# Half of the first token block by plain matmuls, the other half by Strassen after the second block

## The chip, the cores and the metric

The kernel runs on one core of a Trainium2 chip. The core has several engines, each with its own instruction queue that it works through in order: TensorE (PE, matmuls), VectorE (DVE), ScalarE (ACT), GpSimd (POOL) and SyncE (SP, which here only issues DMAs). PE accumulates matmuls in PSUM banks; the other data lies in SBUF, and inputs and outputs in DRAM. The metric is the time of one execution in microseconds (us), less is better.

## The reference

`q`, `k` and `v` are float32 of shape (8 batches, 8 heads, 576 positions, 64); the weights `w_in` (512 x 2048) and `w_out` (2048 x 512) lie in DRAM as float64.

```python
kv  = einsum('bhsd,bhse->bhde', k, v)
out = einsum('bhsd,bhde->bhse', q, kv)
rms = sqrt(mean(out * out, axis=-1, keepdims=True) + 1e-06)
x   = (out / rms * g_norm)       # heads side by side: 4608 tokens x 512
h   = x @ w_in                   # 4608 x 2048
g   = maximum(0.01 * h, h)
return g @ w_out                 # 4608 x 512
```

The two matmuls with the weights are nearly all of the arithmetic.

## The kernel before

**Blocks and chunks.** The 4608 tokens are nine blocks of 512. The hidden width of 2048 is cut into four chunks (`NC`) of 512. A chunk has two halves `h` and two units `u` of 128 columns.

**Block 0 is computed plainly** by `first_block` (L1064): 16 steps, one for each 128 hidden columns. In step n PE does four matmuls for h of that step, ACT applies the leaky relu (L1082), and then PE does four matmuls of the step before into four PSUM accumulators (`o_acc`), so that h_n and o_(n-1) alternate. After the last step the four accumulators are copied to SBUF and written to the output. Both kinds of matmul group are 128 x 128 x 512, at L119 like every matmul; the trace shows a group of four as eight records.

**Blocks 1 to 8 use Strassen's scheme:** seven products of half-size blocks in place of eight, paid for with sums. Block 1 uses one level (`product_h` L877, `product_o` L1000, `strassen` L823): for a chunk seven h products and seven o products, each of four matmuls of 256 columns. POOL makes the sums of weights (`sides_w1` L667, `sides_w2` L689) and of g (`sums_of` L866), DVE and ACT empty PSUM. In block 1 POOL and DVE also build the weights' sums for a second level (`combine` L729), which are written to DRAM; blocks 2 to 8 use two levels (`product_h_two` L957, `Second` L932) and read them back.

**The weights are rounded in the kernel.** Each of 32 jobs (128 hidden columns of one of the two weights) is loaded as raw float64 (`load_w` L281) into one of seven raw homes (`raw_homes` L210) and rounded to float32 by `round_f64` (L230): two conversions on ACT (`add` L248, `cut` L246), a clip on DVE (L250), a sign and exponent step on ACT (L254), a shift and or on DVE (L264), and an integer add of halves on DVE (L267). `add` and `cut` are temporary tiles from the buffers of `gs1` to `gs4`. `round_w` (L295) issues a job up to L254 and lets `finish_w` issue the last two steps later, so that two jobs overlap. Step n of block 0 needs job 2n-1 for h and job 2n+2 for o. In block 0 everything else goes between the steps: `between(n, half)` loads and rounds jobs ahead of their use, and the list `steps` places parts of batch 1's attention.

**Order.** `pin` keeps instructions in the written order on their engine; the activations of g in block 0 (L1082) and some sums are left to a scheduler. The main loop (L1165 on) counts slots, seven for each chunk, and names in lists (`A_SLOTS`, `FINE_SLOTS`, `LAG`) which slot takes a step of the next batch's attention, and how many products the o products trail.

## Time and profile before

| | before |
|---|---|
| median of two runs | 917.43 us (917.01, 917.86) |
| the profiled execution: time, span | 917.86 us, 916.1 us |
| granted PE clock | 1.00 |
| PE busy | 908.9 us (99%) |
| DVE busy | 612.8 us (67%) |
| ACT busy | 345.3 us (38%) |
| POOL busy | 365.8 us (40%) |
| DMA moved | 200.06 MB, mean 218 GB/s |
| first matmul of block 0, first product of block 1 | 23.5 us, 141.2 us |

Busy times are those of one profiled execution, whose own time is 1.8 us above its span. A line of the waits names the engine, the tile it was about to compute, the engine and tile it waited for, the total in us, the number of waits and the longest. A line of the timeline begins with the start and the length in us, then engine, source line, operation, output and inputs, shape and count; in brackets stand the idle time before it and what ended it. PE's matmuls are pipelined, so the distance between two starts tells what a group costs.

### The profile page before, as it was taken

The numbers are of one execution on the slowest core, as the hardware profiler recorded it, in microseconds if no ns is written. First come the engines' busy times: TensorE is split into PE (matmuls) and PEld (weight loads), VectorE is DVE, ScalarE is ACT, GpSimd is POOL, SyncE is SP. The second block draws the span as 40 slices with busy tenths as digits, with TensorE's granted clock in tenths as the row PEclk, the third lists the DMA queues.
The fourth block names the chain that finished last, engine by engine and source line by source line (L and its number), as shares of the span: only waits on it lengthen the run. The fifth ranks groups of instructions, "written<-read, shape, count | busy, mean of one in ns | idle before, by whom it ended". The sixth has DMA issues, their size and how long they took to land.

```text
span 916.1 us, 18019 instructions
## 1 busy us (share of the span) xinstructions
PE 908.9 (99%) x6976; PEld 775.0 (85%) x6976; DVE 612.8 (67%) x1137; ACT 345.3 (38%) x676; POOL 365.8 (40%) x440
## 2 busy tenths in 40 slices
PE   8999999999999999999999999999999999999998
PEld 4444447888998999899999999999999999999997
DVE  5655774587457876587756786678659755755565
ACT  5665643242135233533343324332443333223330
POOL 2000246977633473226321642264226422642222
PEclk9999999999999999999999999999999999999999
DMA  8999918895599778877886789657765676667632
GB/s 258 237 247 222 258 40 252 272 300 167 165 363 286 229 212 266 234 228 217 251 261 217 220 249 271 222 174 221 235 181 178 188 221 198 184 188 224 196 109 93
DMA packets 90229, 200.06 MB, mean 218 GB/s; under 512 B 9888, under 2 KB 42272, under 8 KB 90144
## 3 DMA queue, kind: packets, MB, share of 16 engines
q1 hardware_dynamic: 79680, 187.04, 69.0%
q10 hardware_dynamic: 10016, 10.69, 3.4%
q8 instruction: 56, 0.92, 0.4%
q0 software_dynamic: 448, 1.18, 0.3%
q14 instruction: 29, 0.24, 0.1%
HBM read 172.39 MB, written 26.48 MB: 217 GB/s over the span
## 4 chain that ended last, share of the span: by engine, by line
PE 95%; DMA 2%; DVE 1%; ACT 0%; issue 0%; POOL 0%; ACTq 0%; DVEq 0%; POOLq 0%
PE o_a L119 19%; PE o_c L119 18%; PE h_ha L119 11%; PE h_hb L119 11%; PE h_hc L119 8%; PE h_hd L119 8%; PE o_acc L119 6%; PE h_ps L119 5%; PE o_ps L119 3%; PE h_a L119 2%; PE h_b L119 2%; DMA pairs<-in_moe_w_in_dram 1%; PE h_c L119 1%; PE h_d L119 1%; PE kv_ps L119 1%; DMA pairs<-in_v_dram 1%
## 5 line engine op out<-in xcount | busy, mean ns | idle before, releaser
L663 POOL TENSOR_TENSOR gs<-g 128x512 f32<-128x512 f32 x64 | 81.6, 1276 | 253.8 <-ACT g L859 251.7
L859 ACT ACTIVATE g<-g 128x512 f32<-128x512 f32 x124 | 78.2, 631 | 132.0 <-DVE g L663 132.0
L978 ACT COPY w_all<-h_ha 128x512 f32<-128x512 f32 x84 | 48.8, 582 | 172.9 <-PE h_ha L119 159.8
L119 PE MATMUL o_a<-pairs,gs 128*128 128x256 f32 x384 | 91.3, 381 | 0.0
L119 PE MATMUL o_c<-pairs,gs 128*128 128x256 f32 x376 | 89.2, 380 | 0.0
L663 DVE TENSOR_TENSOR o<-h_hb,o 128x128 f32<-128x128 f32 x104 | 29.9, 287 | 82.9 <-ACT pairs L978 82.8
L119 PEld LDWEIGHTS o_a<-pairs,gs 128*128 128x128 f32 x384 | 69.8, 190 | 9.2 <-POOL pairs L663 1.2
L663 DVE TENSOR_TENSOR o<-o_c,o 128x512 f32<-128x512 f32 (+1 forms) x91 | 61.2, 673 | 23.9 <-PE o_c L119 23.6
L119 PEld LDWEIGHTS o_c<-pairs,gs 128*128 128x128 f32 x376 | 68.3, 190 | 7.6
L663 DVE TENSOR_TENSOR o<-o_a,o 128x512 f32<-128x512 f32 x75 | 51.3, 684 | 28.2 <-PE o_a L119 28.1
L119 PE MATMUL h_ha<-stage,w_all 128*128 128x128 f32 x448 | 59.6, 276 | 0.0
L119 PEld LDWEIGHTS h_ha<-stage,w_all 128*128 128x128 f32 x448 | 56.6, 192 | 3.0 <-issue 0.7
L119 PE MATMUL o_acc<-w,g 128*128 128x512 f32 x128 | 57.8, 595 | 0.8 <-DVE w L267 0.8
L119 PE MATMUL h_ps<-xT,w_all 128*128 128x512 f32 (+1 forms) x136 | 57.8, 570 | 0.0
L663 DVE TENSOR_TENSOR g<-g,pairs 128x512 f32<-128x512 f32 x84 | 55.7, 689 | 1.9
L663 POOL TENSOR_TENSOR pairs<-g 128x128 f32<-128x128 f32 x52 | 23.7, 456 | 76.6 <-PE h_hb L119 48.1
L119 PEld LDWEIGHTS o_acc<-w,g 128*128 128x128 f32 x128 | 24.0, 190 | 31.3 <-issue 28.9
L119 PEld LDWEIGHTS h_ps<-xT,w_all 128*128 128x128 f32 x136 | 25.4, 190 | 28.4 <-issue 25.8
L663 DVE TENSOR_TENSOR w_all<-h_hc,w_all 128x512 f32<-128x512 f32 x56 | 38.4, 685 | 15.9 <-PE h_hc L119 15.8
L663 DVE TENSOR_TENSOR o<-h_hd,o 128x128 f32<-128x128 f32 x78 | 22.1, 284 | 38.0 <-ACT pairs L978 37.9
L119 PE MATMUL h_hb<-stage,w_all 128*128 128x128 f32 x336 | 46.7, 275 | 0.0
L978 ACT COPY pairs<-h_hb 128x384 f32<-128x384 f32 x84 | 39.9, 475 | 14.1 <-PE h_hb L119 13.3
(231 smaller groups left out, 2230.6 us busy)
## 6 DMA issues: line engine op xcount, KB each, us to landing
w_all<-w SPq DMA_DIRECT2D x196, 448.0 KB, 4.2
pairs<-w SPq DMA_DIRECT2D x56, 512.0 KB, 4.4
out_dram<-o ACTq DMA_DIRECT2D x35, 256.0 KB, 4.7
v_in<-in_v_dram SPq DMA_DIRECT2D x29, 288.0 KB, 5.4
k_in<-in_k_dram SPq DMA_DIRECT2D x28, 288.0 KB, 5.1
q_in<-in_q_dram SPq DMA_DIRECT2D x56, 144.0 KB, 6.1
q_in<-in_q_dram SPq DMA_DIRECT2D x56, 140.0 KB, 6.1
w<-stage SPq DMA_DIRECT2D x12, 512.0 KB, 4.6
```

Source lines behind the costliest of these rows:

```text
L119: pin(nc.tensor.matmul(*args, **kw))
L663: ins = eng.tensor_tensor(out_, a, b_, op=ALU.subtract if minus else ALU.add)
L859: nc.scalar.activation(t, t if src is None else src, func=AF.Prelu, alpha=SLOPE)
L978: nc.scalar.copy(q[:, at], bank)
```

## The change

Block 0 computes only its first two chunks plainly (8 steps instead of 16). Its four accumulators are copied to SBUF and stored in a DRAM tile `part` instead of the output. Then block 1 runs all its four chunks by one-level Strassen, and after it block 0's chunks 2 and 3 run by one-level Strassen too, with output tiles that are loaded from `part` (`load_part`) and added to. Blocks 2 to 8 follow as before. The list `units` holds the order of block and chunk.

The weights of chunks 2 and 3 (jobs 16 to 31) are loaded and rounded during block 1, in the slots of `W_SLOTS`; within each chunk the four jobs of `w_in` come first. Their raw homes are three `stage` tiles and the two halves of the tile `early`, and their temporary tiles come from the buffers `k_in` and `v_in` (two each) in place of `gs1` to `gs4`. `rounding` has one more pause ahead of its ACT step (L254 before, L263 after), and `round_w` issues three steps of a job instead of four, so that this step of a job comes after the conversions of the next. The first two pairs of batch 1's k, v and q are loaded ahead of job 7. Batch 1's attention is spread over the first eight steps, batch 2's over slots 22 to 41. The combined weights of the first chunks lie in other tiles (`stage_homes`) before they go to DRAM. In the diff below, places that only replace `n % NC` by `units[n][1]`, limits of loops and the warm-up copies are left out.

```diff
     NC = DF // 2 // (U * P)
+    K = NC // 2
...
-    spare_homes = itertools.cycle(("gs1", "gs2", "gs3", "gs4"))
+    spare_homes = itertools.chain(
+        itertools.islice(itertools.cycle([(gpool, f"gs{i}") for i in range(1, 5)]),
+                         2 * 2 + 2 * 4 * K * U),
+        itertools.cycle([(ins, "k_in"), (ins, "v_in")]))
     def spare(n, name, dtype=F32):
-        return gpool.tile([P, n], dtype, tag=next(spare_homes), name=name)
-
-    raw_homes = itertools.cycle([view(stage, i * NW, NW) for i in range(3)]
-                                + [pair(i, NW) for i in range(4)])
+        pool, tag = next(spare_homes)
+        return pool.tile([P, n], dtype, tag=tag, name=name)
+
+    raws = [view(stage, i * NW, NW) for i in range(3)] + [pair(i, NW) for i in range(4)]
+    raw_homes = itertools.chain(
+        itertools.islice(itertools.cycle(raws), 4 * K * U),
+        itertools.cycle([raws[2], early[:, :NW], early[:, NW:], raws[0], raws[1]]))
...
         if not high_first:
+            yield
             pin(nc.scalar.activation(dst.bitcast(I32), cut, func=AF.Prelu, scale=2.0 ** 90,
...
-    w_jobs[1:-1] = [w_jobs[i + 1 if i % 2 else i - 1] for i in range(1, len(w_jobs) - 1)]
+    n0 = 4 * K * U
+    w_jobs[1:n0 - 1] = [w_jobs[i + 1 if i % 2 else i - 1] for i in range(1, n0 - 1)]
+    for i in range(n0, len(w_jobs), 4 * U):
+        two = w_jobs[i:i + 4 * U]
+        w_jobs[i:i + 4 * U] = two[::2] + two[1::2]
...
     def round_w(j):
         steps = rounding(j)
-        for _ in range(4):
+        for _ in range(3):
             next(steps, None)
         finish_w()
         halfway.append(steps)
...
         for j in range(3, 7):
             load_w(j)
+        for p in range(2):
+            load_pair(1, p)
...
+    units = [(1, c) for c in range(NC)] + [(0, c) for c in range(K, NC)]
+    units += [(i, c) for i in range(2, NB) for c in range(NC)]
+    part_dram = dram.tile([NT, DM], F32, name="part")
...
-    stage_homes = itertools.cycle(range(3))
+    stage_homes = itertools.chain(
+        [view(w1_all, 6 * NW, NW), view(w1_all, 7 * NW, NW),
+         *(w[NC - 1].rearrange("p u n -> p (u n)") for w in w2_sb)] * 2,
+        itertools.cycle([view(stage, i * NW, NW) for i in range(3)]))
...
+    def load_part(os, key):
+
+        os[key] = opool.tile([P, 2, N2], F32, tag="o", name=f"o{key}", bufs=6)
+        r0, c0 = ((int(d) - 1) * N2 for d in key)
+        pin(nc.sync.dma_start(
+            os[key], part_dram[r0:r0 + N2, c0:c0 + N2].rearrange("(t p) m -> p t m", p=P)))
...
         accs = [ps_m.tile([P, DM], F32, tag=t, name="o_acc") for t in ("oa", "oc", "hb", "hd")]
-        x, last = xTs.pop(0), None
-        for n in range(2 * NC * U + 1):
+        x, last = xTs[0], None
+        for n in range(2 * K * U + 1):
             now = last
-            if n < 2 * NC * U:
+            if n < 2 * K * U:
...
-            nc.scalar.dma_start(out[t * P:(t + 1) * P, :], o)
+            nc.scalar.dma_start(part_dram[t * P:(t + 1) * P, :], o)
     first_attention()
-    steps = {i: tail for tail in [tail_of(0, NT, S)] for i in (6, 8, 10)}
-    a_steps = attention(1, False)
-    steps.update((i, a_steps)
-                 for i in (12, 13, 15, 16, 19, 20, 22, 23, 24, 26, 28))
+    tail, a_steps = tail_of(0, NT, S), attention(1, False)
+    steps = {2: [tail], 3: [tail], 4: [tail, a_steps], 11: [a_steps, a_steps]}
+    steps.update((k, [a_steps]) for k in (5, 8, 9, 10, 12, 14))
     loaded, rounded = 7, 5
     def between(n, half):
         nonlocal loaded, rounded
-        go(steps.get(2 * n + half, iter(())), 1)
-
-        while half and rounded < min(3 * n + 8, 2 * n + 13, len(w_jobs) - (n < 11)):
-            if loaded < len(w_jobs):
-                load_w(loaded)
-                loaded += 1
-                if loaded in (15, 19):
-                    load_pair(1, (loaded - 15) // 4)
+        for each in steps.get(2 * n + half, ()):
+            go(each, 1)
+
+        while half and rounded < min(2 * n + 7, n + 10, 4 * K * U + 1):
+            load_w(loaded)
+            loaded += 1
             round_w(rounded)
             rounded += 1
         if half:
             finish_w()
-        if (n, half) == (12, 0):
-            for p in range(2):
-                load_pair(2, p)
     first_block(between)
...
+    while loaded < rounded + 5:
+        load_w(loaded)
+        loaded += 1
...
-    A_SLOTS = (1, 3, 5, 8, 10, 11, 13, 14, 15, 17, 18, 19, 21)
+    W_SLOTS = (1, 2, 4, 5, 7, 8, 10, 11, 12, 13, 14, 15, 16, 17, 18)
+    LATE_ONE = {20: 2, 21: 1}
+    A_SLOTS = {22: 1, 24: 1, 25: 1, 30: 1, 31: 1, 32: 1, 33: 1, 34: 1, 35: 1, 36: 1, 41: 2}
...
+    now, N1 = -1, NC + NC - K
+    rounds = [(1, range(NC)), (0, range(K, NC))] + [(i, range(NC)) for i in range(2, NB)]
+    for i, chunks in rounds:
+        one = i < 2
         steady = not one
-        late, a_steps = a_steps, attention(i + 1, fine=not one) if i + 1 < B else iter(())
+        if i == 1:
+            late, a_steps = a_steps, attention(2)
+        elif i > 1:
+            late, a_steps = a_steps, attention(i + 1, fine=True) if i + 1 < B else iter(())
         os = {}
-        for c in range(NC):
+        for c in chunks:
+            now += 1
+            nxt = units[now + 1] if now + 1 < len(units) else (NB, 0)
             g_sides = {}
             h_steps = product_h(c, h_sides, x_sides, g_sides) if one else \
-                product_h_two(i, c, quarters, g_sides, second_of((i - 1) * NC + c - 2))
+                product_h_two(i, c, quarters, g_sides, second_of(now - 2))
             for t in range(7):
                 slot = 7 * c + t
...
                 if one:
-
-                    if t == 1:
+                    at = 7 * now + t
+
+                    if t == 1 and (i == 0 or c < K):
                         combine(c, 2)
-                    if t == 3 and c < NC - 1:
-                        h_sides, more_h = sides_w1(c + 1)
-                        combine(c + 1, 0)
-                    if t == 5 and c < NC - 1:
+                    if t == 3 and nxt[0] < 2:
+                        h_sides, more_h = sides_w1(nxt[1])
+                        if nxt in ((1, 1), (0, K), (0, K + 1)):
+                            combine(nxt[1], 0)
+                    if t == 5 and nxt[0] < 2:
                         more_h()
-                        combine(c + 1, 1)
-                    if slot == 5:
-                        in_line = True
-                        go(late, 1)
-                        in_line = False
-                    if slot in A_SLOTS:
-                        go(a_steps, 1)
+                        if nxt in ((1, 1), (0, K), (0, K + 1)):
+                            combine(nxt[1], 1)
+                    if at in W_SLOTS:
+                        round_w(rounded)
+                        rounded += 1
+                        if loaded < len(w_jobs):
+                            load_w(loaded)
+                            loaded += 1
+                    else:
+                        finish_w()
+                    if at in (19, 20):
+                        load_pair(2, at - 19)
+                    go(late, LATE_ONE.get(at, 0))
+                    go(a_steps, A_SLOTS.get(at, 0))
                     load_some()
-                    if slot == 24:
-                        go(a_steps)
-                        x_sides, new_quarters, sums, inner = sides_x(i + 1)
+                    if at in (33, 36):
+                        for key in (("11", "12"), ("22", "21"))[at == 36]:
+                            load_part(os, key)
+                    if at == 7 * NC - 4:
+                        x_sides, _, sums, _ = sides_x(0)
                         go(sums)
-                    elif slot == 25:
+                    elif at == 7 * N1 - 4:
+                        x_sides, new_quarters, sums, inner = sides_x(2)
+                        go(sums)
+                    elif at == 7 * N1 - 3:
                         inner(0)
-                    elif slot == 26:
+                    elif at == 7 * N1 - 2:
```

## The prediction

> **What bounds the kernel now.** I read the busy shares first, then the chain that ended last, then TensorE's (PE's) own waits.
>
> ```profile
> PE 908.9 (99%) x6976; PEld 775.0 (85%) x6976; DVE 612.8 (67%) x1137; ACT 345.3 (38%) x676; POOL 365.8 (40%) x440
> PE 95%; DMA 2%; DVE 1%; ACT 0%; issue 0%; POOL 0%; ACTq 0%; DVEq 0%; POOLq 0%
> ```
>
> PE is busy 99% of the span and is 95% of the chain. Its waits in the whole span are five, 4.0 us together; only one lies in block 0's matmuls:
>
> ```profile
> PE o_acc L119 <- DVE w L267: 0.8, 1, 0.8
> ```
>
> So the kernel is one dense stream of matmuls, and two things alone can move it: matmul time added or removed, and new idle time of PE. The clock is 1.00 throughout.
>
> **The matmuls removed and added.** The timeline of PE gives both prices.
>
> ```profile
> 34.95 3.60 PE L119 MATMUL h_ps<-xT,w_all 128*128 128x512 f32 x8
> 38.38 3.60 PE L119 MATMUL o_acc<-w,g 128*128 128x512 f32 x8
> 41.82 3.60 PE L119 MATMUL h_ps<-xT,w_all 128*128 128x512 f32 x8
> ...
> 141.20 1.89 PE L119 MATMUL h_a<-xT,w_all 128*128 128x256 f32 x8
> 142.92 1.89 PE L119 MATMUL h_c<-xT,w_all 128*128 128x256 f32 x8
> 144.65 1.89 PE L119 MATMUL h_a<-xt,pairs 128*128 128x256 f32 x8
> ```
>
> The starts count, since groups overlap: a plain group (four matmuls of 512 columns) takes 38.38 − 34.95 = 3.43 us, a Strassen product 1.73 (mean of two starts). Chunks 2 and 3 leave eight steps of two plain groups: 16 × 3.43 = 54.9 us. They come back as 2 chunks × 14 products × 1.73 = 48.4. Gain **6.5**. The 0.8 us wait above goes too, for the last columns' o_ps now stand before o0 and its rounding is earlier. The profiled execution took 917.86 (span 916.1 and 1.8 around it), 0.4 over the median. Without a new wait the changed kernel would take 917.9 − 7.3 = **910.6**. So a gain of 2% (18 us) is out of reach, and all depends on idle time.
>
> **Where PE must wait.** I followed the changed program's order on each engine, each instruction with what it waits for. Engines run in order, so a matmul waits for all that stands ahead of its producer. Terms are from this trace: a rounding conversion on ScalarE (ACT) 0.56 issue to issue, the sign step L254 0.55 to 0.63, activations of g and PSUM copies 0.5 to 0.6, on VectorE (DVE) L264 0.70, L267 0.69, the clip L250 0.35, a sum from PSUM 0.60, a 512-column operation of GpSimd (POOL) 1.23 to 1.27, DVE to PE 0.15. Rounding gets one more pause: a job's ACT sign step now stands behind the next job's two conversions.
>
> 1. *o2 in block 0.* Its weight is job 6. On ACT, job 6's sign step stands behind g of h3 and job 7's conversions; h3 is the group directly before o2 on PE. From h3's end: 0.5 (g) + 0.56 + 0.60 + 0.63 (ACT) + 0.72 + 0.69 (DVE) + 0.15 = **3.9** idle.
> 2. *h6.* Its weight is job 11, whose conversions stand on ACT behind two squares (0.43 each) and two copies (0.54 each) of batch 1's attention outputs; those matmuls are directly before h6. 1.94 + four conversions (jobs 11 and 12) 2.3 + sign step 0.63 + 1.4 + 0.15 = **6.5**.
> 3. *Chunk 0 of block 1.* The copy of product P1 stands on ACT behind the two issues that store the sums, which wait for DVE copies: 0.8 at P6, and 1.2 at P4 behind rounding: **2.0**.
> 4. *Chunk 1, third product.* It needs POOL's sum of weights, which now stands behind chunk 0's four sums of g; in the old order that sum came first. From the end of chunk 0's last h product: 0.15 + two activations 1.2 + 6 × 1.25 = 8.85, less two products of PE's own, 3.45, is **5.4**.
> 5. *Chunk 1, its last product:* a DVE sum stands behind rounding, which on ACT stands behind a copy of an o product: 3.8 against 3.45 of products: **0.3**.
> 6. *Chunk 2, fourth product.* It needs the DVE sum that empties its bank. That stands behind the sum of the o product directly before it on PE (0.6) and the rest of three jobs. With two temporary buffers a job's conversions wait for the last DVE step of the job two before, so jobs go round the loop conversion, conversion, sign, shift, add: 0.56 + 0.60 + 0.60 + 0.70 + 0.70 = 3.2 each. First job done at 2.4, then two loops 6.4, then the sum 0.6 and 0.15: **9.6**.
>
> From slot 19 on (rounding over) I find no DVE or ACT queue that is late. Sum: 3.9 + 6.5 + 2.0 + 5.4 + 0.3 + 9.6 = **27.7**, which gives 910.6 + 27.7 = **938.3**.
>
> **What I cost at nothing.** DMA: before, its share is 1.0 from 20 to 100 us at about 240 GB/s; 16 raw jobs of 0.5 MB move to the time of block 1, 34 us of transfers at that rate in some 60 us of products. Batch 1's first k, v and q move ahead of job 7 on SP's queue (1.7 MB, 7 us), so job 7 lands near 43, before its 45.9. Part stores (1 MB, four issues on ACT) are counted in item 3; part loads are issued at slots 33 and 36, at least three slots (10 us) before they are read, against 4.4 to 5.4 us for a load of this size. If that cover went, each late transfer would cost PE up to 5 us; it cannot cost below nothing, as no work goes away.
>
> **The unknown cost: DVE beside POOL.** Block 0 of before had an idle POOL until 106 us; rounding ran alone. From then on the timeline shows what both pay:
>
> ```profile
> 106.09 1.51 POOL L663 TENSOR_TENSOR pairs<-w 128x512 f32<-128x512 f32 x1 [99.69 <-ACT cut L246]
> 107.67 1.60 POOL L663 TENSOR_TENSOR pairs<-w,pairs 128x512 f32<-128x512 f32 x1
> ...
> 106.38 1.77 DVE L264 SCALAR_TENSOR_TENSOR w_all<-cut,w_all 128x512 uint32<-128x512 uint32 x1
> 108.18 1.65 DVE L267 CUSTOM_DVE_ANT_0 w_all<-w_all,add 128x1024 uint16<-128x1024 uint16 x1
> 109.75 0.68 DVE L264 SCALAR_TENSOR_TENSOR w<-cut,w 128x512 uint32<-128x512 uint32 x1
> 110.46 0.69 DVE L267 CUSTOM_DVE_ANT_0 w<-w,add 128x1024 uint16<-128x1024 uint16 x1
> ```
>
> The same two steps take 0.69 alone and 1.77 and 1.65 beside POOL: about 1.0 more each. In the changed kernel jobs 11 to 31 are rounded while POOL makes sides and g sums almost without a pause. Bounds, term by term: item 2 has two such steps and POOL starts its sides on the same conversions, 0 to 2.2; o6 and o7 need jobs 14 and 15 with POOL busy, 0 to 3.4; item 4 gives 0 to 2.7 (POOL's six operations at 1.60 to 1.70); item 5 0 to 5.2 (five steps of combining and two jobs ahead of the sum); item 6 has six such steps, 0 to 6.0. Together 0 to 19.5. A gain is excluded: no operation beside another is shorter than alone. POOL pauses between its sums, and of DVE's steps beside it in before some were long and some not (rows above), so I take two fifths, **8**. Forecast 938.3 + 8 = 946.3, say **946**.
>
> [...]
>
> **The rivals.**
> - *All hidden* (chance 0.06): ACT and DVE have slack (38% and 67% busy), the scheduler has placed the waits where their producers are done, and the time is 910.6: not slower, 0.8% faster. It decides if o2, the third product of chunk 1 and the fourth of chunk 2 start without a gap; for it speaks that before has the same kinds of producers and only 0.8 us of waiting in block 0; against it, the orders above, in which the producer starts only after the group directly before ends.
> - *Only half of the waits* (0.14): items 4 and 6, argued from queue order, are partly gone since POOL or DVE run earlier than I walked: 910.6 + 20 = 931, within 2%.
> - *Bare waits, DVE and POOL meeting seldom* (0.27): 938, range 934 to 941.
> - *Forecast, some meetings* (0.33): 946, range 941 to 951.
> - *Full meetings, or one late transfer besides* (0.20): 951 to 963, centre 955: every DVE step beside POOL waits for it; decided by rounding steps of 1.5 us or more in most of block 1.
>
> **How the numbers follow.** The line of 2% (about what a measurement of this kernel can tell from no change) is at 935.8. Slower: 0.33 + 0.20 + most of 0.27 = 0.78. Within: 0.06 + 0.14 and the rest = 0.21. Faster 0.01: no mechanism gives it. The range leaves out all hidden and the top of the last case: 930 to 957.
>
> **What would show it.** PE's waits in the profile after: o_acc on the last rounding step about 4 us in one wait; h_ps about 6.5 in one; an h product of chunk 1 on a POOL sum, 5 or more; an h product of chunk 2 on a DVE sum of g, 9 or more; total PE idle about 30 to 40 us, nearly all before some 220 us. PE's busy time should fall to about 902. DVE's rounding steps of jobs 16 to 31 would show 1.0 us more in a part of cases. The prediction is wrong if those products start without a gap, if PE's busy time doesn't fall, or if gaps come after 230 us, in the two-level blocks, whose order I take as unchanged.

## The result, and the profile after

The changed kernel takes **957.45 us** (median of 955.94 and 958.95) against 917.43: ratio **1.044**, 95% interval 1.036 to 1.051. It is slower by about 40 us. The forecast was 946 with a range of 930 to 957; the sign was right, and the time lies 0.45 us above the upper end of the range. A later measurement of both kernels on one chip gave 955.42 (four runs, 954.49 to 956.66) against 918.55 (seven runs), ratio 1.040 (1.038 to 1.042); this time lies inside the range. So the result is close to the end of the range, but the forecast was some 10 us low, for a cause that it had left out and that the profile and the experiments show.

The readings below are of the execution that took 955.94. Its profile page gives the busy times, the row of the granted PE clock in 40 slices, and the shares of the chain that ended last:

```profile
PE 913.7 (96%) x7072; PEld 797.9 (84%) x7072; DVE 638.1 (67%) x1161; ACT 347.8 (36%) x682; POOL 391.6 (41%) x456
...
PEclk9987988999999999999999999999999999999999
...
PE 78%; DVE 3%; ACT 1%; POOL 1%; issue 1%; DMA 0%; SPq 0%; ACTq 0%; POOLq 0%; DVEq 0%
```

PE's share of the chain that ended last fell from 95% to 78%: the time is no longer set by matmuls alone. The span is 954.2, so PE is idle for 954.2 − 913.7 = 40.5 us instead of 7.2. And PE's busy time did not fall by the 6.5 us of matmul work that went away, it rose by 4.8. The clock row says why: between 48 and 167 us (slices 3 to 7) it has three eights and a seven where before had only nines.

The waits of PE (tile about to be computed, what was waited for, total, number, longest) name the idle time:

```profile
PE h_c L120 <- DVE g L678: 11.5, 1, 11.5
PE h_ps L120 <- DVE w_all L276: 8.0, 1, 8.0
PE h_b L120 <- POOL pairs L678: 7.5, 1, 7.5
PE o_acc L120 <- DVE w L276: 3.8, 1, 3.8
```

They are single waits at four places that the prediction named: the fourth product of chunk 2, h6 of block 0, the third product of chunk 1, and o2 of block 0. Behind them in the list come 1.5 us at the start, as before, and 1.2 at 267 us, the only wait of that size in the two-level blocks.

The timeline of PE at these four places in order of time, each with the group that comes next (start, length, group, idle time before it):

```profile
49.87 6.44 PE L120 MATMUL o_acc<-w,g 128*128 128x512 f32 x8 [3.84 <-DVE w L276]
56.15 3.60 PE L120 MATMUL h_ps<-xT,w_all 128*128 128x512 f32 x8
...
80.34 6.58 PE L120 MATMUL h_ps<-xT,w_all 128*128 128x512 f32 x8 [7.98 <-DVE w_all L276]
86.85 0.98 PE L120 MATMUL o_ps<-qT,kv 64*32 64x448 f32 x16
...
126.77 3.78 PE L120 MATMUL h_b<-xt,pairs 128*128 128x256 f32 x8 [7.50 <-POOL pairs L678]
130.34 2.00 PE L120 MATMUL o_a<-w,g 128*128 128x256 f32 x8
...
168.70 3.35 PE L120 MATMUL h_c<-xt,pairs 128*128 128x256 f32 x8 [11.50 <-DVE g L678]
171.88 1.89 PE L120 MATMUL o_a<-w,g 128*128 128x256 f32 x8
```

The group after each wait is slow. From its start to the next start o2 takes 6.28 us and h6 6.51 (80.34 to 86.85), where a plain group costs 3.43; the products of chunks 1 and 2 take 3.57 (126.77 to 130.34) and 3.18, where a Strassen product costs 1.73. That is 2.85 + 3.08 + 1.84 + 1.45 = **9.2 us** lost beside the waits themselves.

The windows over the first such group and a later stretch (after the stretch: its length, then busy time and count of PE, PE's weight loads, DVE, ACT and POOL, then the granted clock, DMA share and GB/s):

```profile
50.00:56.50 6.50, 6.50 (x9) 2.74 (x10) 6.08 (x9) 4.03 (x7) 3.57 (x4) 0.58 1.04 209
...
172.00:200.00 28.00, 27.49 (x169) 22.93 (x171) 23.24 (x35) 12.20 (x27) 18.69 (x14) 1.00 0.39 122
```

The granted clock is 0.58 in this group, 0.56, 0.50 and 0.56 in the three others, and 1.00 right after the last. In the trace of before no wait lasted over 1.5 us, and its clock is 1.00.

**Where the 38 us went.** Block 2 starts at 264.06 instead of 228.54 us, 35.5 later, and the rest is 2.6 longer, of which 1.9 are waits (1.24 at 267 us, 0.5 and 0.2). The 35.5 are, against before: −6.5 of matmuls, −0.8 for the old wait that is gone, +33.1 of waits, +9.2 of slow groups; together +35.0.

### The profile page after: what moved, and what is told of

Same layout as the page of the kernel before. It is cut to its first block, busy times and chain, and to the rows that moved or that the text cites. A ratio compares the mean times of both kernels' runs of the same rounds, so it can differ in the third digit from the quotient of the medians.

```text
span 954.2 us, 18286 instructions
## 1 busy us (share of the span) xinstructions
PE 913.7 (96%) x7072; PEld 797.9 (84%) x7072; DVE 638.1 (67%) x1161; ACT 347.8 (36%) x682; POOL 391.6 (41%) x456
## 4 chain that ended last, share of the span: by engine, by line
PE 78%; DVE 3%; ACT 1%; POOL 1%; issue 1%; DMA 0%; SPq 0%; ACTq 0%; POOLq 0%; DVEq 0%
PE o_a L120 18%; PE o_c L120 17%; PE h_ha L120 10%; PE h_hb L120 10%; PE h_hc L120 8%; PE h_hd L120 8%; PE o_ps L120 2%; PE h_b L120 1%; PE h_a L120 1%; PE h_d L120 1%; PE h_c L120 1%; DVE g L678 1%; PE kv_ps L120 1%; DVE w L273 1%; POOL stage L678 1%
## 5 line engine op out<-in xcount | busy, mean ns | idle before, releaser
L678 POOL TENSOR_TENSOR gs<-g 128x512 f32<-128x512 f32 x68 | 86.9, 1281 | 307.9 <-ACT g L881 307.9
L120 PE MATMUL o_a<-pairs,gs 128*128 128x256 f32 x408 | 97.0, 381 | 0.0
L120 PE MATMUL o_c<-pairs,gs 128*128 128x256 f32 x400 | 94.9, 380 | 0.0
L678 DVE TENSOR_TENSOR o<-o_c,o 128x512 f32<-128x512 f32 (+1 forms) x98 | 66.0, 674 | 32.4 <-PE o_c L120 26.7
L120 PEld LDWEIGHTS o_a<-pairs,gs 128*128 128x128 f32 x408 | 74.4, 190 | 9.9 <-POOL pairs L678 1.2
L678 DVE TENSOR_TENSOR o<-o_a,o 128x512 f32<-128x512 f32 x82 | 56.1, 684 | 32.8 <-PE o_a L120 28.7
L678 POOL TENSOR_TENSOR gs<-gs,g 128x512 f32<-128x512 f32 x34 | 46.2, 1359 | 2.2
L678 POOL TENSOR_TENSOR gs<-g,gs 128x512 f32<-128x512 f32 x34 | 46.7, 1373 | 0.4
L1000 ACT COPY pairs<-h_hb 128x384 f32<-128x384 f32 x84 | 40.1, 477 | 13.6 <-PE h_hb L120 12.9
L120 PE MATMUL h_hb<-xT,w_all 128*128 128x128 f32 x224 | 43.3, 275 | 0.0
L120 PE MATMUL h_hd<-xT,w_all 128*128 128x128 f32 x224 | 43.3, 275 | 0.0
```

What stands on the lines that cost most here:

```text
L120: pin(nc.tensor.matmul(*args, **kw))
L678: ins = eng.tensor_tensor(out_, a, b_, op=ALU.subtract if minus else ALU.add)
L1000: nc.scalar.copy(q[:, at], bank)
```

## The experiments

The theory after the two traces: (A) each wait costs its own length and besides, where it is long enough, a group or two at a lower clock. Its rivals: (B) these groups are slow for a reason that the wait does not make, such as the work of other engines and DMAs beside them; and, for each single wait, that the next producer in line is nearly as late, so that taking one cause away only moves the wait. Most versions have the time of one execution; it is compared with the profiled execution of the changed kernel, 955.94. The kernel before took 916.9 to 918.6 on the chips used, and executions of the changed kernel 954.49 to 958.95. So a gain of 3 or 4 us in one time says little, and the readings rest on the waits and groups in the traces.

### Does idle time lower the clock? e1_warm, p1_gaps, p2_gaps

`e1_warm` puts matmuls whose sum nobody reads into the four waits, 4, 8, 8 and 12 of them:

```diff
+    def fill(tag, n):
+        idle = ps_m.tile([P, NT], F32, tag=tag, name="fill_ps")
+        x = xTs[0]
+        for _ in range(n):
+            matmul(idle, lhsT=x[:, 0, :P], rhs=x[:, 1, :], start=True, stop=True)
...
+                if n == 6:
+                    fill("hc", 8)
...
+            if n == 3:
+                fill("ha", 4)
...
+                if i == 1 and slot == 9:
+                    fill("ha", 8)
+                if i == 1 and slot == 17:
+                    fill("hd", 12)
```

> The changed kernel with dummy matmuls (128x512, results unused) put on TensorE directly ahead of the four products that wait longest: 4 ahead of o2, 8 ahead of h6, 8 ahead of the third h product of chunk 1, 12 ahead of the fourth of chunk 2. Each takes 0.86 us, so they fit into the waits. Theory A: the matmuls right after a wait of 4 us or more are slow (6.3 to 6.5 us instead of 3.43 for a plain group, 3.6 and 3.2 instead of 1.73 for a Strassen product) because the clock falls while TensorE is idle; filled waits keep the clock at 1.00, the matmuls after them take 3.43 and 1.73, and the time falls by 2.8 + 3.0 + 1.8 + 1.5 = 9 us to about 947 although no wait is shorter. Rival B: the slowness comes with what released the wait (late data, engines beside), not from idleness; the time stays at 956 to 959 or rises by the dummies.

Measured: **951.92**, mean clock 0.998. The timeline of PE (o2, and a later h product of block 1):

```profile
49.60 3.70 PE L120 MATMUL o_acc<-w,g 128*128 128x512 f32 x8 [0.36 <-DVE w L276]
...
175.75 3.34 PE L120 MATMUL h_a<-xt,w_all 128*128 128x256 f32 x8 [2.78 <-DVE g L678]
```

and the window over the groups after the first wait, in the same columns as above:

```profile
50.00:56.50 6.50, 6.50 (x16) 2.85 (x15) 6.12 (x8) 3.99 (x7) 3.67 (x4) 1.00 1.03 241
```

The group after the first filled wait runs at full clock (3.70 instead of 6.44 us; the clock is 1.00 over the other three too), while DVE, ACT, POOL and DMA are as busy beside it as in the row of the changed kernel. That rules out B. The time fell by 4.0, not by 9.2: since PE is now ahead, a DVE sum at 175.75 is late, 2.78 of wait and 1.39 + 0.48 of slow groups behind it.

`p1_gaps` and `p2_gaps` ask the same of the kernel *before*, which has none of the change: POOL doubles g of some steps of block 0 m times, and the activation scales by 2^−m, so that PE waits for POOL in a plain group. The diff is that of `p1_gaps`; `p2_gaps` has `{2: 8, 5: 6, 7: 5, 9: 4}` for the steps and counts.

```diff
-                act = nc.scalar.activation(gT, h_ps, func=AF.Prelu, alpha=SLOPE)
+                m = {2: 4, 4: 5, 6: 6, 9: 8}.get(n, 0)
+                act = nc.scalar.activation(gT, h_ps, func=AF.Prelu, alpha=SLOPE, scale=2.0 ** -m)
                 if n == 2 * NC * U - 1:
                     pin(act)
+                for _ in range(m):
+                    nc.gpsimd.tensor_tensor(gT, gT, gT, op=ALU.add)
```

> The kernel before the change, with the price of a wait measured by itself: behind g of steps 2, 4, 6 and 9 of block 0, chains of 4, 5, 6 and 8 sums of 1.27 us are put on GpSimd, which has nothing else to do there (g is scaled down first, so the result is the same). The o group that reads g starts 3.4 us after its step's g in the old order, so it should wait some 1.5, 3, 4.3 and 6.8 us. Theory A: idle time alone lowers the clock; after the longer waits the next plain groups take up to 3 us more than 3.43, after the shortest nothing is lost, and the time rises by the waits (15 to 16 us) plus 3 to 8 us. Rival B: the groups behind every wait run in 3.43 to 3.5 and the time rises by the waits alone.

Measured: 922.94. Only two of the chains were long enough to stop PE, for 0.41 and 1.99 us, and no group behind them is slow (0.1 us more).

> As the run with waits put into the kernel before, with 8, 6, 5 and 4 sums behind g of steps 2, 5, 7 and 9. Theory A: the loss after a wait goes by its length, with a boundary between 1.5 and 4 us; if the boundary is sharp, waits of one length lose the same in both runs; if the clock's state is taken at fixed times whatever the kernel does, waits of one length lose different amounts, between 0 and 3 us. Rival B: no loss.

Measured: 929.93. PE's timeline around two of its three waits:

```profile
49.76 6.56 PE L119 MATMUL o_acc<-w,g 128*128 128x512 f32 x8 [4.71 <-POOL g L1087]
56.16 3.60 PE L119 MATMUL h_ps<-xT,w_all 128*128 128x512 f32 x8
...
92.43 3.70 PE L119 MATMUL o_acc<-w,g 128*128 128x512 f32 x8 [1.73 <-POOL g L1087]
```

A wait of 4.71 us costs 6.40 − 3.43 = 2.97 more behind it, one of 1.73 nothing. So it takes nothing of the change to get the slow group, only an idle PE.

### One wait at a time: e2_job6, e5_later, e4_homes, c1_three

`e2_job6` issues the last steps of job 6 before job 7's first (the prediction's item 1):

```diff
+        if j == 7:
+            finish_w()
         steps = rounding(j)
```

> The last steps of job 6's rounding are issued ahead of job 7's conversions instead of behind them; nothing else is changed. Theory A (engine order): o2 no longer waits (3.84 before) and the slow matmuls behind it go too (2.8): about 950. Rival: job 6 or its load is late anyway; the wait stays above 3 us and the time at 956 to 959. Third: the time gained is lost again at the next wait, h6, whose wait grows from 8.0 to 11 or more because job 11 is bound by its load and not by the attention outputs ahead of it.

Measured: 952.18 (−3.8). The wait of 3.84 and its slow group are gone, h4 has a new wait of 1.47 with no slow group behind it. Job 6's place on ACT was the cause. The time fell by less than these three come to (5.2), as the slow groups at the other three waits cost 8.0 in this execution where they had cost 6.4.

`e5_later` moves the attention outputs of batch 1, whose squares and copies stand on ACT ahead of job 11, behind h6 (item 2):

```diff
-    steps = {2: [tail], 3: [tail], 4: [tail, a_steps], 11: [a_steps, a_steps]}
-    steps.update((k, [a_steps]) for k in (5, 8, 9, 10, 12, 14))
+    steps = {2: [tail], 3: [tail], 4: [tail, a_steps], 12: [a_steps, a_steps]}
+    steps.update((k, [a_steps]) for k in (5, 8, 9, 10, 13, 14))
```

> Batch 1's attention matmuls and what ScalarE does with them come behind h6 instead of ahead of it; nothing else is changed. Theory A (job 11's conversions stood behind the attention outputs on ScalarE): h6 no longer waits 8.0 us and runs in 3.4 instead of 6.1 to 6.6; about 945 to 947. Rival: job 11's load is late; h6 still waits 5 us or more. Third: the wait moves on to o6, h7 or o7, which need jobs 13 to 15 from the same queue, and 3 us or more of it are found there.

Measured: 947.64 (−8.3). PE's timeline:

```profile
49.65 3.67 PE L120 MATMUL o_acc<-w,g 128*128 128x512 f32 x8 [3.85 <-DVE w L276]
53.16 3.60 PE L120 MATMUL h_ps<-xT,w_all 128*128 128x512 f32 x8
...
70.83 5.40 PE L120 MATMUL h_ps<-xT,w_all 128*128 128x512 f32 x8 [2.37 <-DVE w_all L276]
76.15 0.98 PE L120 MATMUL o_ps<-qT,kv 64*32 64x448 f32 x16
```

h6's wait fell from 7.98 to 2.37, 5.6 less, so item 2's cause is right. In the same lines o2's wait is unchanged at 3.85 but no slow group follows it (3.51), while 2.37 us of wait at h6 cost 5.32 − 3.43 = 1.89 more. About 2.8 of the 8.3 is that missing loss at o2, which the edit does not touch.

The record of the granted clock tells why. In the 14 traces in which it changes between 20 and 280 us, it changes only on a grid of 3.41 us, which does not lie at the same times in each (windows begin at 45.21 us in the changed kernel, at 44.37 in `e5_later`). Windows of this grid around o2, first in the changed kernel, then in `e5_later` (columns as above; the length less PE's busy time is PE's idle time):

```profile
45.21:48.62 3.41, 0.82 (x2) 0.00 (x0) 0.74 (x2) 2.55 (x5) 0.00 (x0) 1.00 0.98 249
48.62:52.03 3.41, 2.16 (x3) 1.16 (x4) 3.31 (x7) 3.23 (x7) 0.00 (x0) 0.50 1.07 264
52.03:55.45 3.42, 3.42 (x5) 1.35 (x5) 3.07 (x5) 2.10 (x4) 2.60 (x3) 0.50 1.07 225
```

```profile
44.37:47.78 3.41, 1.43 (x4) 0.36 (x2) 0.22 (x1) 1.94 (x4) 0.00 (x0) 1.00 1.03 277
47.78:51.19 3.41, 1.54 (x4) 0.86 (x5) 3.25 (x7) 3.22 (x7) 0.00 (x0) 1.00 1.06 257
```

In the changed kernel the first window holds 2.59 us of idle time, and the clock is 0.50 from its end, inside the wait, to 55.45. The same wait in `e5_later` falls on two windows with 1.98 and 1.87, and the clock stays at 1.00. So the loss of this wait, 2.85 and 0.08, depended on how it lay on the grid, which is the case of fixed times in what was expected of `p2_gaps`.

`e4_homes` adds a third pair of temporary buffers to the rounding of jobs 16 to 31 (item 6):

```diff
-        itertools.cycle([(ins, "k_in"), (ins, "v_in")]))
+        itertools.cycle([(ins, "k_in"), (ins, "v_in"), (ins, "k_in"), (ins, "v_in"), (work, "sum0"), (work, "sum1")]))
...
-        return pool.tile([P, n], dtype, tag=tag, name=name)
+        return pool.tile([P, n], dtype, tag=tag, name=name, **({'bufs': 1} if pool is work else {}))
```

> The late rounding gets a third pair of temporary buffers; nothing else is changed. Theory A1, the step as predicted (a job waits for the buffers of the job two before, 3.2 us a turn): the fourth product of chunk 2 waits 3 us less, 8 to 9 instead of 11.5. Theory A2 (what counts is that the sum on VectorE stands behind the steps of three jobs, whatever their buffers): the wait stays at 10.5 to 11.5 and the time at 953 to 959.

Measured: 952.03 (−3.9); the fourth product of chunk 2 waits 8.42 instead of 11.50, less by 3.08: one turn of the loop of 3.2 us. The changed kernel's ACT timeline shows that loop (start, length, conversion, and the wait for the last DVE step of the job two before):

```profile
161.57 0.66 ACT L256 ACTIVATE add<-stage 128x512 uint32<-128x512 uint32 x1 [3.81 <-DVE w_all L276]
...
164.78 0.66 ACT L256 ACTIVATE add<-early 128x512 uint32<-128x512 uint32 x1 [1.48 <-DVE w_all L276]
...
167.99 0.67 ACT L256 ACTIVATE add<-early 128x512 uint32<-128x512 uint32 x1 [1.49 <-DVE w_all L276]
```

`c1_three` makes these three edits together.

> The three edits that each took time off, together: job 6 finished ahead of job 7's conversions, batch 1's attention behind h6, a third pair of temporaries for the late rounding. Theory A (the waits are separate, each with its slow matmuls): the parts add, 956 less 3.8, 8.3 and 3.9 is 940, between 938 and 943, still slower than the kernel before. Rival: the edits uncover waits for loads or for GpSimd, as in the run without late rounding, and 945 or more remain.

Measured: **941.78** (four runs, 940.91 to 942.22), ratio to before 1.027 (1.025 to 1.029). PE's waits that are left:

```profile
PE h_c L120 <- DVE g L680: 8.4, 1, 8.4
PE h_b L120 <- POOL pairs L680: 7.5, 1, 7.5
PE h_ps L120 <- DVE w_all L276: 3.8, 2, 2.4
```

Each edit does here what it did alone: no wait is left at o2, h6 waits 2.39 and the fourth product of chunk 2 8.41, and the third product's 7.50 is untouched. In time the single gains sum to 16.0, or 13.2 without the chance 2.8 in `e5_later`. 955.42 − 941.78 is 13.6, or 12.0 when each is taken against the kernel before on its own chip, so the times agree with separate causes to some 1 us.

### Where the wait only moved: e3_pool, e4_slots, c2_gate

`e3_pool` fixes POOL's order so that the sums of weights come ahead of the four sums of g (item 4):

```diff
-        add(nc.gpsimd, sides[5], a21, a22)
-        add(nc.gpsimd, sides[6], sides[5], a11, True)
+        add(nc.gpsimd, sides[5], a21, a22, pinned=True)
+        add(nc.gpsimd, sides[6], sides[5], a11, True, True)
...
-        add(nc.gpsimd, s1, g21, g22)
...
+        add(nc.gpsimd, s1, g21, g22, pinned=True)
```

(and so for the other three sums of g)

> In block 1 the sums of weights and the sums of g on GpSimd are held in written order, so that chunk 1's weights' sums come ahead of chunk 0's sums of g, as in the kernel before the change. Theory A: the third h product of chunk 1 no longer waits (7.50), and the two products behind it run at 1.73 again (1.8 us more): about 947 to 948 from 956.  Rival: another release takes over (sums of g now late for the o products, or the copy on ScalarE), and half or more of the 7.5 us comes back at the o products of chunk 0.

Measured: 958.96, no gain. The third product's wait went from 7.50 to 0.27, so POOL's order was its cause, but two DVE sums are late next:

```profile
124.97 3.54 PE L120 MATMUL h_d<-xt,pairs 128*128 128x256 f32 x8 [3.01 <-DVE g L678]
...
142.57 3.78 PE L120 MATMUL h_b<-xt,w_all 128*128 128x256 f32 x8 [5.43 <-DVE g L678]
```

These sums stand on DVE behind steps of rounding and of combined weights, which run with one pause of 2.0 from 117 to 143 us and take up to 1.76 us each beside POOL.

`e4_slots` spreads the rounding over more slots of chunks 2 and 3 and loads batch 2's k, v and q later. One sum of chunk 3's weights is then made from a weight that is not yet rounded.

```diff
-    W_SLOTS = (1, 2, 4, 5, 7, 8, 10, 11, 12, 13, 14, 15, 16, 17, 18)
+    W_SLOTS = (1, 2, 4, 5, 7, 8, 10, 11, 14, 16, 17, 18, 19, 20, 21)
...
-    A_SLOTS = {22: 1, 24: 1, 25: 1, 30: 1, 31: 1, 32: 1, 33: 1, 34: 1, 35: 1, 36: 1, 41: 2}
+    A_SLOTS = {25: 1, 26: 1, 27: 1, 30: 1, 31: 1, 32: 1, 33: 1, 34: 1, 35: 1, 36: 1, 41: 2}
...
-                    if at in (19, 20):
-                        load_pair(2, at - 19)
+                    if at == 22:
+                        for p in range(2):
+                            load_pair(2, p)
```

> Fewer weights are rounded ahead of chunk 2's fourth product: from the eighth slot of rounding on they are spread over slots 14 and 16 to 21 instead of 12 to 18; batch 2's first loads and attention steps move three slots to make room. Theory A (the sum on VectorE that this product needs stands behind the rounding of three jobs): its wait falls from 11.5 to 2 or 3 us, and the matmuls after it run at full clock: 944 to 947. Rival: rounding is bound by ScalarE and VectorE in all, and the wait only moves to the products of slots 16 to 21: 954 or more.

Measured: 961.83. The fourth product of chunk 2 waits 1.93 instead of 11.50, but PE waits 6.7 for the later v loads, 4.68 and 4.36 for DVE sums of the next products, each of the last two with a slow group (1.5 and 1.7 more). Spreading the work over more slots put it in the way of later products; the total did not fall.

`c2_gate` is `c1_three` with some of POOL's first sums held until the last weight of chunk 1 is rounded, so that DVE and POOL meet less:

```diff
-        nc.gpsimd.tensor_copy(pair(i, U, 2, 2, P)[:1, 0, 0, r, :1], x_sides[1][:1, 0, :1])
+        nc.gpsimd.tensor_copy(pair(i, U, 2, 2, P)[:1, 0, 0, r, :1], w2_sb[1][K - 1][:1, U - 1, :1])
```

> The same three edits, and GpSimd's first sums of weights start only when the last weight of chunk 1 is rounded, so that rounding in block 0 runs without GpSimd beside it. Theory A (VectorE's rounding steps take 1.1 to 1.8 us beside GpSimd and 0.7 alone): what is left of the wait at h6 (2.4 us and 2 us of slow matmuls) goes, 2 to 5 us less than with the three edits. Rival: GpSimd's sums come too late for chunk 0's third and sixth products, and the time is the same or more.

Measured: 944.03, ratio to before 1.030 (1.028 to 1.032), 2.3 slower than `c1_three`. In the profiled execution (947.30, the longest of the four) three of DVE's four rounding steps from 52.9 to 56.9 us ran at 0.69, but h6's wait grew from 2.39 to 5.29. Job 11's load landed later (its conversion began at 64.03 instead of 61.69 us). The hold also left POOL free for sums of `w_out` weights, and beside these job 11's own two steps took 1.58 and 1.65. Where the held sums ran at last, DVE's steps beside them took 1.21, and a sum behind these gave a new wait of 3.08. So this run does not test what rounding without POOL would be worth at h6.

### What is left without the late rounding: e6_noround, e8_bare, e9_loads

These three replace the rounding of jobs 17 to 31 by one copy on ACT, so that the weights of chunks 2 and 3 are not the rounded ones:

```diff
+            if j > n0:
+                dst, raw = w_jobs[j][0], w_raws.pop(j)
+                pin(nc.scalar.activation(dst, raw.bitcast(F32).rearrange(
+                    "p (a n) two -> p a n two", a=dst.shape[1])[:, :, :, 1], func=AF.Copy))
+                yield
+                return
```

> The rounding of jobs 17 to 31 is left out: one copy on ScalarE stands in for its six steps, so the weights of chunks 2 and 3 are not the rounded ones. Loads, order and all else stay. Theory A: what comes from rounding beside block 1 goes: the wait of chunk 2's fourth product (11.5) and the slow matmuls after it (1.5); GpSimd's six sums ahead of chunk 1's third product take 1.25 each again, so that its wait is 5.4, the bare value of the prediction, instead of 7.5. The waits at o2 and h6 (3.8 and 8.0) stay. About 938 to 940. Rival: GpSimd and the weights' loads bound block 1 with or without rounding: above 948.

Measured: 945.2. The fourth product's wait is gone, as item 6 has it, and the third product's fell from 7.50 to 3.98, below the bare 5.4 of item 4. But PE now comes to the matmuls that read batch 2's v at 181 us instead of 199.7 and waits 6.4 us in two waits for its loads; so the time missed the 938 to 940 that was expected.

`e8_bare` adds the edits of `e2_job6`, `e5_later` and `e3_pool`.

> Three edits together, with the rounding of jobs 17 to 31 left out as in the run without it (so chunks 2 and 3 use weights that are not the rounded ones): job 6 finished ahead of job 7's conversions, batch 1's attention behind h6, weights' sums ahead of the sums of g on GpSimd. Theory A (the matmuls saved are real and the four waits with their slow matmuls are all that stands against them): 911 to 916, faster than the kernel before. Rival: other waits appear or Strassen for two more chunks saves less than 6.5 us: 920 or more.

Measured: 936.89, where 911 to 916 was expected. The v loads cost 11.8 us. SP's queue in the timeline, its longest wait, and the window in which the loads should have run:

```profile
149.52 20.73 SPq L739 DMA_DIRECT2D w<-pairs  x2
170.30 0.42 SPq L132 DMA_DIRECT2D k_in<-in_k_dram  x1
```

```profile
SPq L739 <- POOL pairs L686: 19.9, 1, 19.9
```

```profile
160.00:170.00 10.00, 7.16 (x32) 5.98 (x32) 7.41 (x7) 2.84 (x5) 9.83 (x8) 1.00 0.00 1
```

The DMA engines moved nothing (share 0.00, 1 GB/s) from 160 to 170 us, while the loads stood behind two stores of combined weights whose data POOL, in the order of `e3_pool`, had not made yet.

`e9_loads` issues batch 2's loads at slots 11 and 12, ahead of those stores:

```diff
-                    if at in (19, 20):
-                        load_pair(2, at - 19)
+                    if at in (11, 12):
+                        load_pair(2, at - 11)
```

> The run with three edits and without the late rounding (chunks 2 and 3 use weights that are not the rounded ones), with batch 2's first k, v and q issued eight slots earlier on SP's queue. Theory A (they stood on SP behind stores of weights' sums that wait for GpSimd): the two waits for v, 11.8 us, and the slow matmuls after them go: 920 to 924, the rest over 911 being the other waits of that run, 10 us. Rival: DMA as a whole is behind; the loads of k and v take the place of weights' loads, and 5 us or more come back as a wait for weights: above 927.

Measured: **925.24**, and the v loads cost 0.2. What PE still waits for, from the list of its waits:

```profile
PE h_ps L120 <- DVE w_all L276: 3.8, 2, 2.4
PE o_c L120 <- DVE o L686: 3.2, 2, 2.3
PE o_a L120 <- POOL gs L686: 2.3, 1, 2.3
```

With 0.9 for a POOL sum and 0.6 for an attention output, and without the 1.5 at the start that before has too, that is 10.8, and one slow group of 1.9 stands behind h6. 925.24 − 12.7 = 912.5, 6.0 below the 918.55 of before on that chip; waits under 0.5 us, 1.1 in all, would bring it to 7.1. The working of the prediction has 7.3 (6.5 of matmuls and the old wait). So the saved matmuls are there, and are seen once PE is kept fed; this version leaves the rounding out, and so does not show that the whole kernel could get there.

### The result again, and the best version: r_after, c3_warm

`r_after` is the changed kernel itself, to see how far the clock's part varies between executions.

> The changed kernel once more, against the kernel before. Theory A (waits of fixed length, and a loss of clock after each that differs from run to run): the four waits are again 3.8, 8.0, 7.5 and 11.5 to within 0.1 us, the plain groups and products after them slow by a different sum than 9.2, and single runs spread over 3 us or more, 953 to 960, where the kernel before stays within 2. Rival: the loss is the same in every run, 9.2, and the spread comes from the waits.

Measured: 955.42, waits of 3.84, 7.97, 7.50 and 11.48, slow groups that cost 3.00 + 3.16 + 1.84 + 1.54, with 0.18 in one group more: 9.7. The sum differs from 9.2 as expected, but the spread of single runs is 2.2 us, where 3 or more was expected, and no wider than that of before (2.4).

`c3_warm` is `c1_three` with 2, 8 and 9 of `fill`'s matmuls ahead of h6, the third product of chunk 1 and the fourth of chunk 2.

> The three edits, and dummy matmuls ahead of the three products that still wait: 2 ahead of h6, 8 ahead of the third product of chunk 1, 9 ahead of the fourth of chunk 2. Theory A (after the waits of 2.4, 7.5 and 8.4 us the matmuls lose 2.0, 2.4 and 1.8 us of clock): 5 to 6 us less than with the three edits alone, 935 to 937; part of it may be given back by waits further on, as in the run with all four waits filled. Rival: no gain, 941 to 942.

Measured: 940.14 (four runs, 938.6 to 942.38), ratio to before 1.024 (1.022 to 1.026); clock 1.000, no slow group. Against `c1_three`, which ran on another chip, the ratio to before fell by 0.33%, some 3 us, where its slow groups had cost 1.89 + 1.84 + 0.45 + 1.61 = 5.8; a wait of 2.06 at an o product and one of 2.26 at the attention outputs came in their place. By its ratio it is the fastest version of the changed kernel that computes the whole reference, though its single times overlap with those of `c1_three`, and no version tried beats the kernel before.

## Why the prediction was right or wrong, step by step

| step of the prediction | forecast, with its bounds | measured |
|---|---|---|
| 1, o2 | 3.9 | 3.84 |
| 2, h6 | 6.5 + 0 to 2.2 | 7.98 |
| 3, chunk 0 | 2.0 | 1.46 (0.60 + 0.86) |
| 4, third product of chunk 1 | 5.4 + 0 to 2.7 | 7.50 |
| 5, last product of chunk 1 | 0.3 + 0 to 5.2 | 0.43 |
| 6, fourth product of chunk 2 | 9.6 + 0 to 6.0 | 11.50 |
| o6 and o7 | 0 to 3.4 | none |
| sum of waits | 27.7 + 8 = 35.7 | 32.7 |
| from slot 19 on | none | 2.3 |
| slow groups after waits | no term | 9.2 |

- **The matmul balance (−6.5) and the old wait (−0.8)** held: the start of block 2 is explained to 0.5 us with them, and `e9_loads` comes to 6 or 7 less than before once its waits are taken off.
- **The six waits** came where they were forecast. For the four long ones the causes named are shown: `e2_job6`, `e5_later`, `e4_homes` and `e3_pool` each removed or shortened one by undoing its cause. The two small items were not tested. The sum was 3.0 too high.
- **The unknown cost of DVE beside POOL** was taken at 8. Items 2, 4 and 6 together are 5.5 over their bare sums, and the traces show the meetings; DVE first (items 2, 4 and 6 in order of time) and POOL at item 4 after it, in the changed kernel:

```profile
77.40 1.76 DVE L273 SCALAR_TENSOR_TENSOR w_all<-cut,w_all 128x512 uint32<-128x512 uint32 x1
79.19 1.10 DVE L276 CUSTOM_DVE_ANT_0 w_all<-w_all,add 128x1024 uint16<-128x1024 uint16 x1
...
118.95 1.64 DVE L273 SCALAR_TENSOR_TENSOR w_all<-cut,w_all 128x512 uint32<-128x512 uint32 x1
120.62 1.63 DVE L276 CUSTOM_DVE_ANT_0 w_all<-w_all,add 128x1024 uint16<-128x1024 uint16 x1
...
163.33 0.69 DVE L273 SCALAR_TENSOR_TENSOR w_all<-cut,w_all 128x512 uint32<-128x512 uint32 x1
```

```profile
123.34 1.71 POOL L678 TENSOR_TENSOR pairs<-w_all 128x512 f32<-128x512 f32 x1
125.12 1.59 POOL L678 TENSOR_TENSOR pairs<-pairs,w_all 128x512 f32<-128x512 f32 x1
```

  Job 11's two steps ahead of h6 cost 1.76 + 1.10 instead of 1.4, which is the 1.5 that item 2 lies over its bare sum. Around 120 us both sides pay, DVE 1.6 instead of 0.69 and POOL 1.6 to 1.7 instead of 1.25; at 163 us, in the long wait of item 6, POOL is mostly idle and DVE runs at 0.69. So item 6 took 1.9 of its 6.0. From 100 to 182 us only 6 of the 28 shift and add steps in the trace took 1.5 us or more: the rival *Full meetings* has the measured time in its band of 951 to 963, but not by what it named. No run shows that every DVE step beside POOL waits for it: in the rows above DVE's steps grow by 0.4 to 1.1, less than a POOL sum of 1.25, and POOL's grow too, by 0.3 to 0.5.
- **DMA at nothing** held for the changed kernel: of its waits none of 0.4 us or more is put down to a transfer. `e6_noround` and `e8_bare` show the cover that was named there: without the wait of 11.5, batch 2's loads cost 6.4 and 11.8 us.
- **From slot 19 on** 2.3 us were missed: 0.4 at 194 us, and in the two-level blocks, whose order was taken as unchanged, 1.24, 0.5 and 0.2.
- **The step that failed** is the one at the head: "two things alone can move it: matmul time added or removed, and new idle time of PE. The clock is 1.00 throughout." It gave a matmul after a wait of 4 to 11 us the price of one in a dense stream. The runs put a third term there: 9.2 us in the changed kernel (9.7 when measured again). With it the same working gives 946.3 − 3.0 + 2.3 + 9.2 = 954.8, against 955.94 measured. The 3.0 of waits that were forecast too high hid part of the missing term. This is also why "PE's busy time should fall to about 902" was wrong: slow matmuls count as busy, and it was 913.7. A busy time that does not fall was one of the prediction's own signs of being wrong, and so were gaps after 230 us.

The trace of before could not price the term, as its longest wait is 1.5 us. Two things in it pointed that way and were not asked about: a clock row of nothing but nines beside a kernel with hardly any wait, and the matmuls into `idle_ps`, which nobody reads, at its start (the helper is named `keep_warm`). Neither of the two gives a price; the 1.45 to 3.08 us behind each of the four waits came only with the runs.

What stays open: where the grid of the clock lies in a given execution, and so what a single wait of 2 to 4 us costs beforehand. The added pause in the rounding was not undone alone, so its own price is not known.

## What to carry to other kernels

When a change opens gaps in a dense stream of matmuls, price each gap of some 2.4 us or more (2.37 is the shortest that slowed a group here) as its length plus the 1.4 to 3.2 us that the groups behind it lost here, and look for that term where PE's busy time rises though its work fell. Follow the order on each engine to the instruction that a wait is for: that gave the place and nearly the length of all four waits from the old trace and the new order alone. And before a cause is taken away, ask which producer is late next: several of the edits here only moved a wait, as rounding, weights' sums and loads all had to pass through the same stretch before 200 us.

## What the runs showed of the hardware

**A wait lowered the clock in these runs by how it lay on a grid of 3.41 us.** At the groups of PE whose usual length is known, waits from 1.45 to 2.33 us (15 of them) cost at most 0.2 more behind them. Waits from 2.37 to 11.7 us cost 1.4 to 3.2 in the group behind them and the one after it, with no trend to more for the longest, except the 3.85 in `e5_later` that cost 0.08. The granted clock was 0.50 to 0.58 over the four such groups of the changed kernel, and 0.68 over one that was slow in part (h6 of `e5_later`).

The clock records of those 14 traces show what lies behind these numbers. Every stretch at 0.50 is 1, 2, 3 or 4 windows of 3.41 us long; in the changed kernel they last 6.83, 10.24, 6.83 and 10.24 us. At the end of a window at 1.00 the clock fell in all 45 cases in which PE had been idle for 2.02 us or more of it (2.02 in `e6_noround`; 2.59 and three times 3.41 in the changed kernel), and in none with 1.98 (`e5_later`) or less. It rose again at the end of a window with up to 0.52 us of idle time, and not with 0.79 or more; of two with 0.61 it rose in one, that of the changed kernel at 171.50. The loss came to about half of what was left at 0.50 once the matmuls went on: for o2 (55.45 − 49.87) / 2 = 2.8, against 2.85 measured. An estimate from these numbers: a single wait under 2 us costs only its length, as one window then holds no more than the 1.98 that left the clock at 1.00; one over some 4 us, twice 1.98, costs more. The longest that cost nothing more was the 3.85 in `e5_later`, and 3.98 in `e6_noround` cost 1.78.

**A queue that waited held up the loads behind it while DMA stood still:** in `e8_bare` 20.73 us on SP for two stores, with nothing moved (share 0.00) from 160 to 170 us.
